# Moving one weight fetch, two pieces of product and some conversion steps in a fused attention and expert kernel

## The chip, the cores and the metric

The program runs on one core of a Trainium2 chip. The metric is device time in microseconds. The kernel before took a median of 728.87 us in three runs (727.69 to 729.34). Five engines work side by side, each through its own list of instructions in order: TensorE (PE, with its weight loads PEld), VectorE (DVE), ScalarE (ACT), GpSimd (POOL) and SyncE (SP), which here only issues DMAs. An instruction waits until the semaphores that it names have been reached, and everything behind it on its engine waits with it.

## The reference

Three stages, each fed by the one before. q, k and v have 2 batches of 8 heads, 768 rows and 64 columns; the gated layer has 512 inputs and 1536 hidden columns; there are 8 experts of 512 x 1024.

```python
# 1: attention; a row sees the rows of its own hash bucket
q_bits = (einsum('bhsd,dk->bhsk', q, proj) > 0); k_bits likewise
scores = where(q_bucket == k_bucket, q @ k.T / sqrt(D), -1e9)
attn = softmax(scores);  x = (attn @ v), heads side by side: 1536 x 512
# 2: gated layer
x = (x @ w_a) * (x @ w_b) @ w_out
# 3: each row goes to the one expert with the highest routing logit
out[mask] = gate_w[mask, None] * (relu(x[mask] @ w1[e]) @ w2[e])
```

## The kernel before

**Attention** runs in 48 units (NU = 48): 16 heads, three units each, a unit being two strips of 128 rows against all 768 columns. In the loop over u (`for u in range(NU + 2)`), unit u has its row maxima (L213, VectorE), exponentials (L219, ScalarE), normalisation (L231, GpSimd) and, two passes later, its 32x32 turn (L238, VectorE). TensorE makes the scores of the next unit (L205, L208) and then one of: half of a head's product with v (`pv`, L250, 48 matmuls that the trace shows as 96 records), the turning or signing of the next pair's q and k, or filler. The scores use two PSUM buffers (tag s), so those of the next strip wait for the exponential of the one before. Units 42 to 47 are the last pair of heads, 14 and 15.

**Filler** is the gated layer's first chunk. A piece is `gated_products(...)` for one half of the inner dimension, six matmuls of 128x384 (L536); two pieces make one product, whose result is read by L545 (ScalarE) or by L549, L550 and L551 (VectorE, ScalarE, GpSimd). `fill` tells in which pass how many pieces run. In passes 40, 43 and 46 they use PSUM banks of pv, later ones a buffer of the scores (then the output is named part). Until pass NU + 1 the reading steps are held back to the next pass's hook 2, behind its turn.

**Weights** of that chunk arrive as 64-bit numbers and are converted by `split64`: a fetch on SP (L431) and seven steps. With `scratch`, as here, these are rest (L436, VectorE), top (L439, VectorE), low (L445, ScalarE), add (L450, GpSimd), size (L455, ScalarE), guard (L461, VectorE) and parts (L466 on ScalarE, L467 on GpSimd). `outs` are the two halves of w_out. Both go through the tile late, which lies in the single buffer of raw, where the last pair's q and k had been loaded; the second half's fetch waits until the first half is converted. `plan` holds each fetch, `places` the passes of the seven steps.

The place within a pass is set by the hooks: in `hook(u, at)`, at 3 and 2 stand before and after the turn, 0 behind TensorE's work of the pass, 1 behind the fetch of v (`load_v`, four DMAs, L94), 4 at the end. Behind the loop the code goes on with hooks of passes NU + 2 to NU + 4, between which stand the two halves of head 15's product.

**Afterwards** the gated layer's products run chunk by chunk (ab, L536; yp, L568), the router is woven in, and the experts follow (hp, hr and op). SP fetches the next weights (raw) as buffers come free; the first of these, w_a, stands right behind late in its list. yp is the first product that reads the converted w_out.

The order of all instructions is that of the Python code: what a hook calls is put into each engine's list at that point.

Of the kernel before, what the change touches and what calls it, by code (L numbers as in the profile page):

```python
# [1030 lines left out]
def tile_kernel(ctx, tc, q, k, v, proj, w_a, w_b, w_out, emb, tau, w1, w2, out, dbg=None):  # L1031
    K = Kernel(tc, q, k, v, proj, w_a, w_b, w_out, emb, tau, w1, w2, out)
# [4 lines left out]
    with tc.manual_schedule():  # L1037
        const = ctx.enter_context(tc.tile_pool(name="const", bufs=1, side="left"))
        X = Experts(K, const)
# [12 lines left out]
        NU = B * H * (S // 256)  # L1052
        with tc.tile_pool(name="conv", bufs=1, side="left") as X.conv, \
                tc.tile_pool(name="att", bufs=2, side="right") as sb, \
                tc.tile_pool(name="ps_s", bufs=2, space=PSUM) as ps_s, \
                tc.tile_pool(name="ps_pv", bufs=1, space=PSUM) as ps_pv:

            def spare():
                return X.mid.tile([128, 4 * 384], F32R, tag="g", name="spare")

            def late():
                return sb.tile([128, 2 * S], F32, tag="raw", name="late", bufs=1)

            jobs = [X.load_first(w, f, spare) for f in range(2) for w in range(2)]
            outs = [X.load_first(2, f, late) for f in range(2)]


            plan = {(-1, 0): [jobs[0][0], jobs[1][0]], (36, 1): [outs[0][0]], (45, 1): [outs[1][0]]}
            places = (
                (3, 4, 5, 6, 6, 7, 9), (8, 8, 9, 10, 12, 13, 15), (16, 17, 18, 21, 21, 22, 27), (20, 23, 24, 28, 30, 31, 33),  # L1070
                (38, 38, 39, 40, 41, 41, 45), (NU, NU, NU, NU + 1, NU + 1, NU + 1, NU + 2),
            )
            for (_, steps), us in zip(jobs + outs, places):
                for m, u in enumerate(us):
                    plan.setdefault((u, 3 if m in (3, 4, 6) else 4), []).append(steps[m])
            plan[13, 0], plan[16, 0] = [jobs[2][0]], [jobs[3][0]]
            first = [(t, f, w, h) for t in range(2) for f in range(2) for w in range(2) for h in range(2)]


            fill = {40: 2, 43: 2, 46: 2, NU: 2, NU + 2: 2, NU + 3: 2, NU + 4: 4}  # L1080

            held = []

            def hook(u, at):
                if at == 2:
                    while held:
                        held.pop(0)()
                for job in plan.pop((u, at), []):
                    job()
                if at == 0:  # L1090
                    for n in range(fill.get(u, 0)):
                        t, f, w, half = first.pop(0)
                        if half == 0:
                            X.part = K.banks[(2, 0)[n // 2]] if u < NU else K.bank()
                        X.gated_products(0, t, f, w, half, X.part, held if u < NU + 2 else None)

            K.attention(X.xh, X.xl, (sb, ps_s, ps_pv), hook)
            assert not plan and not first
        pctx = ExitStack()
# [188 lines left out]
```

## Time and profile before

| | |
|---|---|
| median of three runs | 728.87 us (727.69 to 729.34) |
| profiled execution | 727.76 us |
| its span, first to last instruction | 726.0 us |
| PE busy | 697.9 us, 96% |
| PEld busy | 586.9 us, 81% |
| DVE busy | 459.0 us, 63% |
| POOL busy | 415.5 us, 57% |
| ACT busy | 354.1 us, 49% |
| mean share of DMA time of the bulk queue q1 | 37.5% |

The span lies 1.8 us under the execution's time. Times in the rows are from the span's start. Busy shares are means over stages that differ: up to some 232 us the attention runs, with filler, and behind it the gated layer and the experts. "Idle before" in a row is the time in which that engine did nothing before that instruction, and the name behind the arrow is what the profile takes to have ended the wait, which is inferred; "issue" means that it found nothing waited for.

### The profile page before, as it was taken

What the parts mean: (1) busy time and instruction counts of PE and PEld (TensorE: products, weight loads), DVE (VectorE), ACT (ScalarE), POOL (GpSimd) and SP (SyncE); (2) the same over time, 40 slices, a digit from 0 to 9 for tenths busy, and PEclk for the clock granted to TensorE, in tenths of its full rate; (3) what the DMA queues carried; (4) which work ended last, traced back from release to release, by engine and by line L of the source; (5) the groups of instructions that cost most, each with busy time, mean ns of one, the idle gap of its engine ahead of it and who ended that gap; (6) DMA issues with size and microseconds to landing.
All of it is one profiled execution on the core that took longest, in us unless ns stands there. A gap on an engine that the chain in (4) does not pass through costs nothing.

```text
span 726.0 us, 16193 instructions
## 1 busy us (share of the span) xinstructions
PE 697.9 (96%) x6793; PEld 586.9 (81%) x6793; DVE 459.0 (63%) x669; ACT 354.1 (49%) x658; POOL 415.5 (57%) x343
## 2 busy tenths in 40 slices
PE   7799999997989999999999999999999999999996
PEld 5455656564768989999999999998889899889995
DVE  3999999997984535646545556434744855555650
ACT  3778888886753342222121212143446556556551
POOL 0668778875773563745646626545424766656651
PEclk9999999999999999999999999999999999999999
DMA  6948744633341230311111301443332866577510
GB/s 143 220 111 177 162 119 117 164 84 98 71 133 60 72 105 5 113 59 58 59 60 59 112 4 59 157 162 116 113 134 79 290 215 219 196 240 241 202 54 23
DMA packets 68603, 88.29 MB, mean 122 GB/s; under 512 B 28963, under 2 KB 41123, under 8 KB 68528
## 3 DMA queue, kind: packets, MB, share of 16 engines
q1 hardware_dynamic: 63888, 78.71, 37.5%
q0 software_dynamic: 2560, 7.34, 2.7%
q10 hardware_dynamic: 2080, 1.18, 0.5%
q8 instruction: 54, 0.88, 0.5%
q14 instruction: 21, 0.17, 0.1%
HBM read 75.52 MB, written 7.34 MB: 114 GB/s over the span
## 4 chain that ended last, share of the span: by engine, by line
PE 77%; DVE 10%; ACT 5%; issue 3%; DMA 3%; POOL 1%; SPq 1%; POOLq 0%; DVEq 0%
PE ab L536 24%; PE yp L568 13%; PE op L912 11%; PE hp L862 10%; PE pv L250 6%; PE st L205 4%; DVE nm L213 4%; DVE et L238 3%; ACT e L219 3%; PE part L536 2%; PE hr L880 2%; PE xgt L839 1%; PE pv L536 1%; PE st L208 1%; DMA raw<-in_k_dram 1%
## 5 line engine op out<-in xcount | busy, mean ns | idle before, releaser
L536 PE MATMUL ab<-xh,w 128*128 128x384 f32 x704 | 185.7, 338 | 0.0
L536 PEld LDWEIGHTS ab<-xh,w 128*128 128x128 f32 x704 | 127.7, 188 | 2.1 <-issue 1.2
L231 POOL TENSOR_SCALAR e<-e,s,mc 128x768 f32<-128x768 f32 x96 | 93.8, 988 | 46.3 <-ACT e L219 38.2
L536 PE MATMUL ab<-xl,w 128*128 128x384 f32 x352 | 118.3, 336 | 0.0
L551 POOL TENSOR_TENSOR g<-a,g 128x384 fp32r<-128x384 f32 x48 | 56.4, 1176 | 107.2 <-ACT g L550 107.2
L818 POOL TENSOR_TENSOR w<-raw,w 128x1024 fp32r<-128x1024 f32 x36 | 88.0, 2447 | 39.2 <-ACT w L817 37.7
L568 PE MATMUL yp<-w,g 128*128 128x512 f32 x432 | 103.3, 391 | 1.0 <-DVE a L549 0.7
L219 ACT ACTIVATE e<-st,nm 128x768 f32<-128x768 f32 x96 | 85.8, 898 | 36.4 <-DVE r L223 25.7
L213 DVE TENSOR_REDUCE nm<-st 128x1 f32<-128x768 f32 x96 | 89.5, 937 | 11.2 <-PE st L208 10.8
L568 PEld LDWEIGHTS yp<-w,g 128*128 128x128 f32 x432 | 80.3, 188 | 16.6 <-DVE a L549 1.0
L205 PE MATMUL st<-ks,qs 64*128 64x384 f32 x192 | 83.7, 516 | 9.4 <-ACT e L219 9.1
L205 PE MATMUL st<-k,q 64*128 64x384 f32 x192 | 84.2, 519 | 4.6 <-ACT e L219 4.5
L238 DVE STREAM_TRANSPOSE et<-e 128x1536 f32<-128x1536 f32 x48 | 84.9, 1768 | 0.0
L912 PE MATMUL op<-w,hth 128*128 128x512 f32 x256 | 80.7, 397 | 0.0
L862 PE MATMUL hp<-xgh,w 128*128 128x256 f32 x448 | 80.7, 281 | 0.0
L250 PEld LDWEIGHTS pv<-et,vr 32*64 32x64 f32 x3072 | 60.7, 132 | 20.5 <-issue 11.1
L550 ACT CAST g<-a 128x384 fp32r<-128x384 f32 x48 | 24.7, 515 | 107.8 <-DVE a L549 107.8
L250 PE MATMUL pv<-et,vr 32*64 32x192 f32 x3072 | 72.7, 329 | 4.3 <-issue 2.3
L818 DVE TENSOR_TENSOR w<-raw,w 128x1024 fp32r<-128x1024 f32 x28 | 64.9, 2319 | 14.6 <-ACT w L817 14.3
L862 PEld LDWEIGHTS hp<-xgh,w 128*128 128x128 f32 x448 | 69.2, 188 | 0.3
L545 ACT COPY a<-ab 128x384 f32<-128x384 f32 x44 | 20.9, 476 | 95.6 <-PE ab L536 94.4
L536 PEld LDWEIGHTS ab<-xl,w 128*128 128x128 f32 x352 | 66.2, 188 | 0.8
(201 smaller groups left out, 1232.2 us busy)
## 6 DMA issues: line engine op xcount, KB each, us to landing
raw<-in_moe_w_dram SPq DMA_DIRECT2D x32, 1024.0 KB, 5.2
vr<-in_v_dram SPq DMA_DIRECT2D x64, 192.0 KB, 3.8
raw<-in_moe_w_a_dram SPq DMA_DIRECT2D x5, 1024.0 KB, 5.3
raw<-in_moe_w_b_dram SPq DMA_DIRECT2D x5, 1024.0 KB, 5.1
raw<-in_moe_w_out_dram SPq DMA_DIRECT2D x5, 1024.0 KB, 5.0
raw<-in_k_dram SPq DMA_DIRECT2D x16, 192.0 KB, 4.8
qs<-q SPq DMA_DIRECT2D x16, 192.0 KB, 3.7
raw<-in_q_dram SPq DMA_DIRECT2D x14, 192.0 KB, 4.1
```

The source lines that it names most:

```text
L205: nc.tensor.matmul(st[:, n, :H2], q[d, ql], k[d], start=True, stop=False, tile_position=(64 * n, 0))
L213: nc.vector.tensor_reduce(NM[u][:, t:t + 1], ST[u, t][:, :, :H2], axis=AX.XY, op=ALU.max, negate=True)
L219: nc.scalar.activation(halves(E[u][:, t]), ST.pop((u, t))[:, :, :H2], AF.Exp, bias=NM[u][:, t:t + 1], accum_out=SU[u][:, t:t + 1])
L231: nc.gpsimd.tensor_scalar(E[u][:, t], E[u][:, t], r[:, t:t + 1], c[:, t:t + 1], ALU.mult, ALU.add)
L238: nc.vector.transpose(ET[h][:, :, 2 * g:2 * g + 2].rearrange("p b c s -> p c b s"), E.pop(u).rearrange("p c (b s) -> p c b s", s=32),)
L250: nc.tensor.matmul(pvb[a // 2][m:m + 64, a % 2, :NC * 32], v[d], et[d, n].rearrange("p c s -> p (c s)"), start=(n < 2), stop=(n >= NB32 - ...
L536: nc.tensor.matmul(p[:, :384], w[:, k, fs], x[:, k, cols], start=(k == 0 and n == 0), stop=(k == self.KD - 1 and n == 2),)
L551: nc.gpsimd.tensor_tensor(gl[:, f], a, f32(gh[:, f]), ALU.subtract)
L568: nc.tensor.matmul(p, g[:, f, rows], w[:, f], start=(n == 0), stop=(n == 5))
L818: eng.tensor_tensor(l, raw, f32(h), ALU.subtract)
L862: nc.tensor.matmul(p[:, :256], w[:, k, fs], x[:, k], start=(n == 0), stop=(n == 3 * self.KD - 1))
L912: nc.tensor.matmul(p, h[:, 2 * n + f, rows], w[:, f], start=(n == 0 and f == 0 and m == 0), stop=(n == 3 and f == 1 and m == 2),)
```

## The change

In `tile_kernel`, five entries of tables change. The fetch of the first half of w_out goes from pass 36 to pass 35, and its first step, rest, from pass 38 to 37. The second half's steps top, low, add, size, guard and parts go one pass later each, its step rest and its fetch stay. Of the filler, the two pieces of pass NU + 2 go to pass 47, with a buffer of the scores as output; the pieces are taken in the same order as before, so pass 47 now runs those that pass 48 had, and pass 48 those that pass 50 had.

```diff
-            plan = {(-1, 0): [jobs[0][0], jobs[1][0]], (36, 1): [outs[0][0]], (45, 1): [outs[1][0]]}
+            plan = {(-1, 0): [jobs[0][0], jobs[1][0]], (35, 1): [outs[0][0]], (45, 1): [outs[1][0]]}
...
-                (38, 38, 39, 40, 41, 41, 45), (NU, NU, NU, NU + 1, NU + 1, NU + 1, NU + 2),
+                (37, 38, 39, 40, 41, 41, 45), (NU, NU + 1, NU + 1, NU + 2, NU + 2, NU + 2, NU + 3),
...
-            fill = {40: 2, 43: 2, 46: 2, NU: 2, NU + 2: 2, NU + 3: 2, NU + 4: 4}
+            fill = {40: 2, 43: 2, 46: 2, 47: 2, NU: 2, NU + 3: 2, NU + 4: 4}
...
-                            X.part = K.banks[(2, 0)[n // 2]] if u < NU else K.bank()
+                            X.part = K.banks[(2, 0)[n // 2]] if u < NU - 1 else K.bank()
```

On SP, at the last pair's swapped copies (ks, qs) and the fetch of head 12's v (vr), the lists differ so:

```order
 L106 DMA ks<-k 64x384 x2
 L104 DMA qs<-q 64x768 x2
+L431 DMA late<-in_moe_w_out_dram 128x1024
 L94 DMA vr<-in_v_dram 32x4x384 x4
-L431 DMA late<-in_moe_w_out_dram 128x1024
 L175 DMA qg<-qf 64x384 x2
 L94 DMA vr<-in_v_dram 32x4x384 x12
```

The fetch of late went from behind the four vr to ahead of them.

On VectorE, from the turn (L238) of unit 35 over pass 38 to the first row maximum of unit 39, before the change:

```order
L238 STREAM_TRANSPOSE et<-e 128x2x24x32
L213 TENSOR_REDUCE nm<-st 128x1
L223 RECIPROCAL r<-su 128x2
L213 TENSOR_REDUCE nm<-st 128x1
L229 SCALAR_TENSOR_TENSOR s_2744<-nm,r 128x2
L238 STREAM_TRANSPOSE et<-e 128x2x24x32
L436 TENSOR_SCALAR late<-late 128x512
L439 SCALAR_TENSOR_TENSOR late<-late 128x512
L213 TENSOR_REDUCE nm<-st 128x1
```

The same place after it:

```order
L238 STREAM_TRANSPOSE et<-e 128x2x24x32
L436 TENSOR_SCALAR late<-late 128x512
L213 TENSOR_REDUCE nm<-st 128x1
L223 RECIPROCAL r<-su 128x2
L213 TENSOR_REDUCE nm<-st 128x1
L229 SCALAR_TENSOR_TENSOR s_2745<-nm,r 128x2
L238 STREAM_TRANSPOSE et<-e 128x2x24x32
L439 SCALAR_TENSOR_TENSOR late<-late 128x512
L213 TENSOR_REDUCE nm<-st 128x1
```

L436, which reads what was fetched, went from behind the turn of unit 36 to behind that of unit 35; L439 stayed.

On TensorE, from head 14's products (L250) to the first filler matmul behind head 15's first half, the order's difference is (a filler product is 12 matmuls in nine such rows, part is its PSUM tile; the rows of filler in the middle are as they were):

```order
-L250 MATMUL pv<-et,vr 64x192 x96
+L250 MATMUL pv<-et,vr 64x192 x48
 L536 MATMUL part<-xh_98,w 128x384
 L536 MATMUL part<-xl_100,w 128x384
...
-L536 MATMUL part<-xh_98,w 128x384 x2
+L536 MATMUL part<-xh_98,w 128x384
+L250 MATMUL pv<-et,vr 64x192 x48
+L536 MATMUL part<-xh_98,w 128x384
```

Of the 24 filler matmuls that stood behind both halves of head 14, 12 now stand between the halves.

## Rows read from the trace of the kernel before

**Rows 1.** The page: engine, busy us (share) xinstructions; then one group of L250.

```profile
PE 697.9 (96%) x6793; PEld 586.9 (81%) x6793; DVE 459.0 (63%) x669; ACT 354.1 (49%) x658; POOL 415.5 (57%) x343
...
L250 PE MATMUL pv<-et,vr 32*64 32x192 f32 x3072 | 72.7, 329 | 4.3 <-issue 2.3
```

**Rows 2.** Stretches: from:to, length, busy us of each engine, PEclk, DMA share, GB/s.

```profile
170.00:174.00 4.00, 0.48 (x4) 0.35 (x6) 3.61 (x7) 1.52 (x3) 0.43 (x1) 1.00 0.01 1
174.00:180.00 6.00, 6.00 (x114) 3.50 (x112) 4.68 (x6) 3.52 (x9) 4.33 (x6) 0.72 0.01 3
212.00:214.50 2.50, 0.40 (x18) 0.38 (x20) 2.47 (x3) 0.00 (x0) 1.82 (x2) 1.00 0.09 31
214.50:219.50 5.00, 5.00 (x32) 4.72 (x20) 1.52 (x3) 2.77 (x6) 0.34 (x1) 0.66 0.01 3
232.50:726.00 493.50, 486.63 (x2867) 447.41 (x2867) 261.61 (x384) 186.63 (x314) 260.91 (x148) 1.00 0.36 118
```

**Rows 3.** Timeline of VectorE: start us, us, instruction, idle before and its releaser.

```profile
140.59 0.94 DVE L213 TENSOR_REDUCE nm<-st 128x1 f32<-128x768 f32 x1
...
151.77 0.96 DVE L213 TENSOR_REDUCE nm<-st 128x1 f32<-128x768 f32 x1 [0.31 <-PE st L208]
...
161.28 1.77 DVE L238 STREAM_TRANSPOSE et<-e 128x1536 f32<-128x1536 f32 x1
163.36 0.96 DVE L213 TENSOR_REDUCE nm<-st 128x1 f32<-128x768 f32 x1 [0.31 <-PE st L208]
...
170.36 0.43 DVE L436 TENSOR_SCALAR late<-late 128x512 int32<-128x512 int32 x1 [3.35 <-DMA qg<-qf]
...
180.28 0.96 DVE L213 TENSOR_REDUCE nm<-st 128x1 f32<-128x768 f32 x1 [1.38 <-PE st L208]
```

**Rows 4.** Timeline of SP's DMA issues: start us, us, DMA.

```profile
156.63 1.19 SPq L104 DMA_DIRECT2D qs<-q  x2
162.42 1.74 SPq L94 DMA_DIRECT2D vr<-in_v_dram  x4
164.20 0.43 SPq L431 DMA_DIRECT2D late<-in_moe_w_out_dram  x1
...
205.69 0.39 SPq L431 DMA_DIRECT2D raw<-in_moe_w_a_dram  x1
```

**Rows 5.** DMA from issue to landing: of qs, 157 to 160 us; of late.

```profile
qs<-q SPq DMA_DIRECT2D x2, 192.0 KB, 2.9
...
DMA to landing us min/median/max: 5.7/5.7/5.7
```

**Rows 6.** Chain of waits, 207 to 226 us: start us, us, what.

```profile
207.96 3.80 PE pv L250 x168
211.77 2.33 issue
214.10 0.87 PE pv L250 x20
214.96 5.94 PE part L536 x24
...
223.04 2.28 PE part L536 x12
```

**Rows 7.** DMA queues, 211 to 212 us: packets, MB, share of 16 engines.

```profile
q1 hardware_dynamic: 187, 0.37, 95.4%
q8 instruction: 1, 0.02, 6.1%
```

**Rows 8.** Instructions on tile late: duration ns min/median/max, first and last start us.

```profile
L436 DVE TENSOR_SCALAR late<-late x2: 427/748/1069, 170.4 to 211.0; 128x512 int32<-128x512 int32 x2
L439 DVE SCALAR_TENSOR_TENSOR late<-late x2: 694/1026/1357, 170.8 to 212.1; 128x512 int32<-128x512 int32 x2
```

**Rows 9.** Timelines of ScalarE and VectorE behind head 14's product.

```profile
215.01 0.48 ACT L270 COPY xp<-pv 64x384 f32<-64x384 f32 x1 [3.33 <-PE pv L250]
...
218.60 0.56 DVE L549 TENSOR_TENSOR a<-part,a 128x384 f32<-128x384 f32 x1 [3.48 <-PE part L536]
```

## The prediction

> **What bounds the kernel now.** I read the page's first section, then the table of stretches, then each engine's timeline around the two places that the diff touches, and the chain of waits last. TensorE is busy for 697.9 of 726.0 us [rows 1], and after 232.5 us for 486.63 of 493.5 us, at full clock [rows 2]. So what the attention stage saves is kept only if the later work shifts as a block; it can, since its first engine steps stand behind the attention's last ones, and TensorE is the engine that they feed. The attention stage has two holes in TensorE. In 170 to 174 us it is busy for 0.48 us, and in 212 to 214.5 us for 0.40 us; behind each hole comes a stretch at a granted clock of 0.72 and 0.66, between the two levels 1.2 and 2.4 GHz, so part of it ran at the low one [rows 2].
>
> The first hole comes from VectorE. Behind the turn of unit 36 (L238) it stands idle for 3.35 us and then runs L436 on tile late [rows 3]. The releaser in that row is qg, but L436 reads late: its fetch was issued at 164.20 us, behind the four vr fetches that SP could start only at 162.42 us [rows 4], and the late fetch whose landing is recorded took 5.7 us [rows 5]; 164.20 + 5.7 = 169.9, just ahead of 170.36. The next row maximum (unit 39) stands behind L436 and L439, so scores, exponentials and TensorE stop. Price: the first row maxima of units 32 and 35 start at 140.59 and 151.77 us, 11.18 us for three units; those of units 38 and 41 at 163.36 and 180.28 us, 16.92 us [rows 3]. The hole, its low clock and the two inserted steps cost 5.74 us.
>
> The second hole lies inside the products L250 of head 14: 168 of them, 2.33 us in which the row names nothing that was waited for ("issue"), then 20 more [rows 6]. In 211 to 212 us the bulk queue fills the 16 engines to 95.4% and one block of 16 KB passes on the instruction queue [rows 7]: the 1 MB of raw was issued at 205.69 us, next on SP behind the second late [rows 4]. I read the hole as TensorE waiting for its own code behind this traffic; over the whole program L250 has 2.3 us of such idle time, so this is the only one [rows 1]. It costs 2.33 us; the slow clock behind it makes 24 first-product matmuls take 5.94 us where 12 take 2.28, so 5.94 - 2 x 2.28 = 1.38 us, and 20 L250 take 0.87 instead of 20 x 3.80/168 = 0.45, so 0.42 us [rows 6]. Together 4.13 us.
>
> **The change part by part.** *Fetch a unit sooner.* In SP's order late now stands ahead of the four vr and right behind the two qs, which SP has issued by 156.63 + 1.19 = 157.8 us [rows 4]. vr loses nothing: it cannot start before 162.42. The landing is bounded by the rows of qs (2.9 us, 192 KB) and late (5.7 us, behind vr) [rows 5]: 160.7 to 163.5 us. L436 moved with it, to behind the turn of unit 35, which ends at 161.28 + 1.77 = 163.05 us [rows 3]. So its wait is 0 to 0.5 us; I take 0, since in the new place no vr is ahead of it.
>
> *L436 and L439 stay on VectorE*, now in two units. They cost 0.43 to 1.07 and 0.69 to 1.36 us [rows 8], the upper ones beside a busy GpSimd, less the 0.31 us that VectorE was idle at 163.36 us [rows 3]: 0.8 to 2.1 us. GpSimd is at work in both new places, and the unit's other engines have some slack, so I take 1.3. First term: 5.74 - 1.3 = 4.4 us, from 5.74 - 2.1 - 0.5 = 3.1 to 5.74 - 0.8 = 4.9.
>
> *Two pieces brought between the halves.* Twelve matmuls of 128x384 move from behind the second half of head 14's products to between its halves. The work is the same (five groups of 12 and four halves before yp, then as now), so all of the gain is the hole. TensorE ran the 168 L250 from 207.96 us; the first half has 92 of them left, to 207.96 + 92 x 0.0226 = 210.04 us. The pieces add 2.28, to 212.32. The code that was missing came at 214.10 us. If TensorE meets the same instruction count, it does so 12 matmuls earlier in the products: 160 instead of 172 of 192, that is 64 x 0.0226 = 1.45 us into the second half, at 213.77. The hole shrinks to 0.33 us, and with so short an idle I expect no low clock. Second term: 4.13 - 0.33 = 3.8 us. It can't be over 4.13; below, the fetch may be asked for later and land up to 1.2 us later, half of the room that the pieces fill: 2.6.
>
> What could be late next there: (a) The first half of head 15 needs the turn of unit 47. VectorE now runs L549 (0.56 [rows 9]) on the moved pieces, L436 (up to 1.07) and the turn (1.77 [rows 3]): 212.4 + 0.56 + 1.07 + 1.77 = 215.8 us. (b) It needs ScalarE's four copies L270 of head 14 (0.48 each [rows 9]): 214.82 + 1.95 = 216.8 us. TensorE gets to it at 214.10 + 32 x 0.0226 + 2.28 = 217.1 us with the next pieces. Both are covered, (b) by 0.3 us only. If (b) came later, TensorE would wait as long as it does.
>
> *Conversion steps of the second half* (L439, L445, L450, L455, L461) go a unit later. They and the two that make w from them work on 128x512 elements each; at L439's upper duration five of them in a row are 5 x 1.36 = 6.8 us [rows 8], and from the copies' end at 216.8 they would be done by 223.6. yp, which needs them, starts behind 217.1 + 2 x 2.17 + 3 x 2.28 = 228.3 us at the earliest. So I cost them at nothing; 4.7 us hide them, and what is over would delay yp. L439 now stands behind the turn of unit 47, which spares (a) its 0.69 to 1.36 us.
>
> *outs of the first half*: its L436 is the only step of it that moves.
>
> **Rule and row.** The row shows 2.33 us of TensorE idle with nothing waited for, and a code block passing amid a full bulk queue [rows 6, 7]. The Trainium skill, "Runtime: NRT & Kernel Launch", Instruction fetch mechanics, says that instructions come in 16 KiB blocks through a queue of the sequencer's own, and that crossing a block is mostly hidden. The trace agrees with the size (0.02 MB); with "mostly hidden" it would disagree if my reading holds. By that rule the hole is something else, which the pieces need not shrink; that is the first rival below.
>
> **Sum.** 4.4 + 3.8 = 8.2 us, and the later stage shifts whole. The profiled execution took 727.76 us, span 726.0, so it would take 719.6. It is 1.1 us below the median 728.87; against the median the forecast is 728.87 - 8.2 = 720.7 us. The forecast's own range: terms 3.1 to 4.9 and 2.6 to 4.13, so 5.7 to 9.0 us, 719.8 to 723.2; down to 718.7 if the profile's 1.1 us belong to the kernel.
>
> **Rivals.**
> Hole stays: if the 2.33 us and the slow clock come wherever TensorE runs a stretch of L250 there, only the first term is left: 728.87 - 4.4 = 724.5. For it: the row names no releaser. Against: it is the only one in 3072 products [rows 1], exactly when the bulk queue is full.
> Wait moves along: L436 stands a unit earlier as well; if late lands at 167 us, VectorE waits as long as before and only the second term is left: 728.87 - 3.8 = 725.1. For it: the load is 512 KB behind two qs. Against: [rows 5] bound the landing by 163.5.
> Change does nothing that shows: both of these, 728.9.
> Slower: code starves TensorE oftener. late now travels beside qs, right ahead of vr, and the 1 MB raw still follows the second late, with 12 more matmuls between TensorE and its next block. [rows 7] show what bulk on all engines can do to one block. Each hole costs 4.1 us as above. With the first two gone and three new ones the time is 728.87 - 8.2 + 3 x 4.1 = 733.0; from two on the change is no gain. Against: sixteen heads' vr were fetched, and L250 shows a single hole [rows 1].
>
> **How the numbers follow.** Forecast 0.66, hole stays 0.14, wait moves 0.08, nothing 0.07, slower 0.05. The first three are faster by over 0.2% (1.5 us, about what a measurement of this kernel can tell): 0.88; within it 0.07; slower 0.05. The range 718.7 to 725.2 takes in the first three.
>
> **What would show it.** After: L436 of the first half with under 0.6 us of idle before it, and the row maxima of units 38 and 41 some 12.5 us apart; granted clock 1.00 where it was 0.72. At the end: 12 first-product matmuls between two groups of 96 L250, and an "issue" of under 0.5 us in the second; yp starting some 8 us earlier than 232.5; about 493.5 us from there to the end. I am wrong if an idle of over 2 us stands in L250 again, if L436 waits over 2 us, or if the stage behind yp is over 1 us longer.

## The result, and the profile after

The changed kernel takes a median of 718.09 us in six runs (717.45 to 721.46); the kernel before, in six runs that include the three shown above, 727.97 us (724.78 to 729.34). The ratio is 0.988, with a 95% interval of 0.9849 to 0.9911: faster by some 9 us, where 8.2 us and a time of 720.7 us were forecast. The median lies 0.6 us below the forecast's range (718.7 to 725.2), which was worked out from the first three runs' 728.87 us; the ratio on that median gives 720.1 us, and the gain stands at the upper end of the 5.7 to 9.0 us forecast. The profiled execution took 717.86 us, its span is 716.1 us, 9.9 us under that of before.

The page after, engine by engine and the group L250, answers to [rows 1]:

```profile
PE 693.9 (97%) x6793; PEld 584.1 (82%) x6793; DVE 461.4 (64%) x669; ACT 353.8 (49%) x658; POOL 414.8 (58%) x343
...
L250 PE MATMUL pv<-et,vr 32*64 32x192 f32 x3072 | 71.7, 326 | 2.0 <-ACT q L128 1.9
```

L250 no longer has the 2.3 us of "issue". Stretches after (columns as in [rows 2]), around the two places and from yp's start on:

```profile
160.00:180.00 20.00, 19.35 (x376) 12.13 (x361) 19.79 (x29) 17.05 (x36) 15.40 (x20) 1.00 0.42 106
200.00:223.50 23.50, 22.74 (x456) 19.67 (x456) 13.68 (x21) 10.91 (x23) 13.07 (x14) 1.00 0.43 130
223.50:716.00 492.50, 486.06 (x2867) 447.51 (x2867) 264.58 (x384) 186.54 (x314) 260.38 (x148) 1.00 0.36 119
```

TensorE works for 19.35 of 20 us and 22.74 of 23.5 us, at full clock, where it had the two holes and a granted clock of 0.72 and 0.66. Behind yp's start it does the same 486 us of work. VectorE's timeline, to be held against [rows 3]:

```profile
151.44 0.96 DVE L213 TENSOR_REDUCE nm<-st 128x1 f32<-128x768 f32 x1 [0.31 <-PE st L208]
...
160.94 1.77 DVE L238 STREAM_TRANSPOSE et<-e 128x1536 f32<-128x1536 f32 x1
162.74 0.71 DVE L436 TENSOR_SCALAR late<-late 128x512 int32<-128x512 int32 x1
163.37 0.94 DVE L213 TENSOR_REDUCE nm<-st 128x1 f32<-128x768 f32 x1
...
166.92 1.06 DVE L439 SCALAR_TENSOR_TENSOR late<-late 128x512 int32<-128x512 int32 x1
...
175.13 0.96 DVE L213 TENSOR_REDUCE nm<-st 128x1 f32<-128x768 f32 x1
```

The rows at 163.37 and 175.13 us are the first maxima of units 38 and 41: 11.76 us apart, where it was 16.92. L436 has no idle time before it. SP's issues after, which answer to [rows 4]:

```profile
156.31 1.19 SPq L104 DMA_DIRECT2D qs<-q  x2
157.60 0.54 SPq L431 DMA_DIRECT2D late<-in_moe_w_out_dram  x1
162.08 1.74 SPq L94 DMA_DIRECT2D vr<-in_v_dram  x4
...
200.54 0.39 SPq L431 DMA_DIRECT2D raw<-in_moe_w_a_dram  x1
```

The view of the tile does not tell when this fetch landed after the change. It does so for the same fetch in the kernel after with a store (one of the experiments below), where it was issued at 157.34 us (KB, then us from issue to landing):

```profile
late<-in_moe_w_out_dram SPq DMA_DIRECT2D x1, 512.0 KB, 5.0
```

By that, late landed at about 157.60 + 5.0 = 162.6 us; in the trace of after itself the semaphore of this fetch was last raised at 162.56 us. That lies inside the 160.7 to 163.5 us forecast, but only 0.15 us ahead of the end of unit 35's turn at 160.94 + 1.77 = 162.71 us, behind which L436 starts. The chain of waits at the end of the attention, for [rows 6]:

```profile
202.81 2.20 PE pv L250 x92
205.01 2.28 PE part L536 x12
207.29 2.34 PE pv L250 x96
209.63 2.28 PE part L536 x12
211.91 2.13 PE pv L250 x96
...
218.47 4.38 PE part L536 x24
...
223.56 4.38 PE yp L568 x18
```

Twelve matmuls of filler stand between head 14's two halves, no "issue" is left, and 24 of filler take 4.38 instead of 5.94 us. The second half takes 2.34 us where the next takes 2.13: that is what is left of the hole. The code block still passes amid a full bulk queue; the DMA queues from 206 to 207 us, as in [rows 7]:

```profile
q1 hardware_dynamic: 191, 0.38, 97.5%
q8 instruction: 1, 0.02, 6.5%
```

**Where the 9.9 us came from.** I cut both traces at the first row maximum of units 35, 38, 41 and 47 and at yp's first matmul; the last three columns are from the experiments below. All in us:

| stretch | before | after | fetch and rest | pieces | steps |
|---|---|---|---|---|---|
| start to unit 35 | 151.77 | 151.44 | 151.02 | 151.22 | 152.00 |
| units 35 to 38 | 11.59 | 11.94 | 11.94 | 11.59 | 11.59 |
| units 38 to 41 | 16.92 | 11.76 | 11.76 | 18.10 | 16.41 |
| units 41 to 47 | 24.05 | 24.04 | 24.02 | 24.02 | 24.02 |
| unit 47 to yp | 28.22 | 24.38 | 27.96 | 24.90 | 26.40 |
| yp to the end | 493.43 | 492.51 | 492.41 | 492.64 | 492.24 |

The first hole gave 16.92 - 11.76 - 0.35 = 4.81 us, the second 28.22 - 24.38 = 3.84. Both are figures of one pair of executions: other traces that keep the first hole (pieces, steps and, below, the store in the kernel before) took 18.10, 16.41 and 17.36 us for units 38 to 41, by which it is worth 4.3 to 6.0 us. The other 1.25 us stand in the first and the last stretch. The start varies by 1 us between these traces without a change that reaches it, and the end is as short with the steps alone, which win nothing that can be measured; so I don't count them to the change.

### The profile page after: what moved, and what is told of

Same layout as the page of the kernel before. It is cut to its first block, busy times and chain, and to the rows that moved or that the text cites. A ratio compares the mean times of both kernels' runs of the same rounds, so it can differ in the third digit from the quotient of the medians.

```text
span 716.1 us, 16191 instructions
## 1 busy us (share of the span) xinstructions
PE 693.9 (97%) x6793; PEld 584.1 (82%) x6793; DVE 461.4 (64%) x669; ACT 353.8 (49%) x658; POOL 414.8 (58%) x343
## 4 chain that ended last, share of the span: by engine, by line
PE 78%; DVE 11%; ACT 4%; issue 3%; DMA 3%; SPq 0%; POOL 0%; POOLq 0%; DVEq 0%
PE ab L536 25%; PE yp L568 14%; PE op L912 11%; PE hp L862 10%; PE pv L250 5%; DVE nm L213 5%; PE st L205 4%; DVE et L238 4%; ACT e L219 2%; PE hr L880 2%; PE part L536 2%; PE xgt L839 1%; PE pv L536 1%; PE st L208 1%; DMA raw<-in_k_dram 1%
## 5 line engine op out<-in xcount | busy, mean ns | idle before, releaser
L551 POOL TENSOR_TENSOR g<-a,g 128x384 fp32r<-128x384 f32 x48 | 51.4, 1070 | 102.5 <-ACT g L550 102.3
L238 DVE STREAM_TRANSPOSE et<-e 128x1536 f32<-128x1536 f32 x48 | 84.9, 1768 | 0.0
L250 PEld LDWEIGHTS pv<-et,vr 32*64 32x64 f32 x3072 | 59.7, 130 | 17.6 <-issue 8.2
L250 PE MATMUL pv<-et,vr 32*64 32x192 f32 x3072 | 71.7, 326 | 2.0 <-ACT q L128 1.9
```

The lines of the kernel that those rows point to most:

```text
L238: nc.vector.transpose(ET[h][:, :, 2 * g:2 * g + 2].rearrange("p b c s -> p c b s"), E.pop(u).rearrange("p c (b s) -> p c b s", s=32),)
L250: nc.tensor.matmul(pvb[a // 2][m:m + 64, a % 2, :NC * 32], v[d], et[d, n].rearrange("p c s -> p (c s)"), start=(n < 2), stop=(n >= NB32 - ...
L551: nc.gpsimd.tensor_tensor(gl[:, f], a, f32(gh[:, f]), ALU.subtract)
```

## The experiments

My theory: there are two holes apart from each other, the first of VectorE waiting for late, the second of TensorE waiting for its own code behind bulk traffic; the fetch heals the one, the pieces heal the other. The rivals: qg, which the profile names, held VectorE; moving the steps did it; the second hole belongs to that run of products, whatever the traffic.

The diffs show parts of the changed lines.

**Fetch and rest alone.**

```diff
-(36, 1): [outs[0][0]]
+(35, 1): [outs[0][0]]
-(38, 38, 39, 40, 41, 41, 45)
+(37, 38, 39, 40, 41, 41, 45)
```

> Only the first half's fetch (pass 36 to 35) and its step rest (38 to 37). Theory (two separate holes, each part of the change removes one): the first hole goes, 4.8 us of the trace's 9.9 us; ratio about 0.9935; the issue hole inside L250 of head 14 stays at 1.5 to 2.5 us, yp starts 4.5 to 5.5 us earlier than 232.5. Rival (the two holes are one story, the late start of attention's end makes the second): the second hole shrinks too, and the gain is 7 us or more.

720.96 us against 726.8 (the median of before in this and the next three experiments), ratio 0.9914 [0.9899, 0.9930]. Units 35 to 41 go as after, to 0.01 us. The gain is above what I expected: 0.9935 lies outside the interval, and yp started at 226.69 us, 5.85 us sooner; beyond the first hole the trace is shorter in the start, behind unit 47 and behind yp (table), where the edit moves nothing. The second hole comes earlier by the time saved, and stays whole; its chain of waits:

```profile
202.38 3.80 PE pv L250 x168
206.18 2.08 issue
208.26 0.87 PE pv L250 x20
209.12 5.93 PE part L536 x24
```

So the holes are independent.

**Pieces alone.**

```diff
-fill = {40: 2, 43: 2, 46: 2, NU: 2, NU + 2: 2, NU + 3: 2, NU + 4: 4}
+fill = {40: 2, 43: 2, 46: 2, 47: 2, NU: 2, NU + 3: 2, NU + 4: 4}
-X.part = K.banks[(2, 0)[n // 2]] if u < NU else K.bank()
+X.part = K.banks[(2, 0)[n // 2]] if u < NU - 1 else K.bank()
```

> Only the two pieces, brought between the halves of head 14's product. Theory: the first hole stays as before (L436 idle 3 to 3.5 us before it), the second shrinks to under 0.5 us; 3.4 to 3.9 us less, ratio about 0.995. VectorE now has L549, L436 and L439 ahead of the turn of unit 47, which may cost up to 0.5 us of it. Rival (the hole comes wherever TensorE runs L250 there): an issue of about 2.3 us stands in L250 again, ratio 1.000.

722.84 us, 0.9940 [0.9925, 0.9955]. The first hole stays (18.10 us from unit 38 to 41), the second shrinks to 0.47 us in the chain:

```profile
210.76 2.28 PE part L536 x12
213.04 1.49 PE pv L250 x64
214.52 0.47 issue
214.99 0.91 PE pv L250 x32
215.90 2.28 PE part L536 x12
```

The hole now comes after 64 products of the second half, the place where 0.33 us of idle were worked out. Before the break TensorE ran 92 + 12 + 64 = 168 matmuls, and in [rows 6] 168 as well: the break goes by the count of instructions, so the 12 of filler bring it 12 products earlier. Counted from the program's start, the break stands before the same matmul, the 3655th recorded, in before and in every experiment that has it in L250. The queue of the blocks carries 54 of them in each trace, one for some 252 of TensorE's 2 x 6793 matmuls and weight loads [rows 1]: that it is TensorE's own code is read from these counts.

**Conversion steps alone.**

```diff
-(NU, NU, NU, NU + 1, NU + 1, NU + 1, NU + 2),
+(NU, NU + 1, NU + 1, NU + 2, NU + 2, NU + 2, NU + 3),
```

> Only the second half's conversion steps a pass later. Theory: hidden, ratio 0.999 to 1.001, both holes as before. Rival (they are what lets the turn of unit 47 and so head 15 come earlier): 1 us or more less on their own.

725.54 us, 0.9989 [0.9975, 1.0003]: no difference that can be told. Both holes stand. In its chain, though, the filler behind the second one is quick:

```profile
211.47 2.08 issue
213.55 0.87 PE pv L250 x20
214.42 4.36 PE part L536 x24
```

```profile
213.50:219.00 5.50, 5.45 (x60) 4.90 (x68) 2.02 (x3) 3.47 (x8) 1.01 (x1) 1.00 0.01 3
```

The second fence is the stretch behind that hole: its granted clock is 1.00. So a hole of this length is followed by a low clock in some executions and not in others; with the low clock the same 24 matmuls took 5.94 us, 1.58 more. What decides it stays open. And the 20 products took 0.87 us at full clock too, so that this part of the price isn't the clock's.

**Rest alone**, the rival that qg was the releaser: L436 a pass sooner with the fetch where it was.

```diff
-(38, 38, 39, 40, 41, 41, 45)
+(37, 38, 39, 40, 41, 41, 45)
```

> Only the step rest a pass sooner, with its fetch left behind the four vr. Theory (VectorE's order with the landing of late is the first hole): L436 now waits in pass 37 until about 170 us, for some 6.5 to 7 us, ahead of the row maximum of unit 38; 2 to 4 us slower, ratio 1.003 to 1.006. Rival (what ended the wait was qg's landing, as the row named it): L436 now stands ahead of the qg fetch in the program, so the wait goes and 4 us are gained.

730.62 us, 1.0041 [1.0027, 1.0056]: slower. VectorE's timeline, and late's fetch, which was issued at 163.68 us (us to landing last):

```profile
170.72 0.43 DVE L436 TENSOR_SCALAR late<-late 128x512 int32<-128x512 int32 x1 [8.19 <-DMA late<-in_moe_w_out_dram]
...
late<-in_moe_w_out_dram SPq DMA_DIRECT2D x1, 512.0 KB, 6.8
```

L436 starts at 170.72 us, as in [rows 3], though it stands a unit sooner in the list: the landing of late, at 163.68 + 6.8 = 170.5 us, sets it, not qg. The idle time grew to 8.19 us, more than the 6.5 to 7 expected.

**Fetch alone**, with rest where it was.

```diff
-(36, 1): [outs[0][0]]
+(35, 1): [outs[0][0]]
```

> Only the first half's fetch a pass sooner, its step rest left in pass 38. Theory (the landing was all that the first hole waited for): as with rest moved too, within 0.6 us of it: ratio 0.990 to 0.994, L436 without idle before it, second hole as before. Rival (moving L436 a pass ahead was needed): half of the gain or less.

723.41 us against 726.71 (the median of before here and in the rest), 0.9958 [0.9943, 0.9972]. VectorE no longer waits for late, but does both steps in one unit:

```profile
166.93 0.82 DVE L436 TENSOR_SCALAR late<-late 128x512 int32<-128x512 int32 x1
167.79 1.37 DVE L439 SCALAR_TENSOR_TENSOR late<-late 128x512 int32<-128x512 int32 x1
169.08 0.94 DVE L213 TENSOR_REDUCE nm<-st 128x1 f32<-128x768 f32 x1
```

TensorE's timeline shows what that costs: 1.21 us of idle before the next scores, where after has 0.38.

```profile
171.16 0.59 PE L205 MATMUL st<-ks,qs 64*128 64x384 f32 x1 [1.21 <-ACT e L219]
```

From unit 38 to 41 it takes 12.94 us, with rest moved as well 11.76, less 0.35 in the three units before: 0.83 us by the traces. The second hole stayed, at 2.30 us. My expectation of within 0.6 us of fetch and rest together missed: the move of rest spreads the two steps over two units. The rival's "half of the gain or less" isn't met by the medians either: 3.30 us against 5.84. The medians and the spans (721.6 and 719.1) differ by 2.5 us, though; the other 1.7 stand in the start (151.78 against 151.02), unit 47 to yp (28.16 against 27.96) and behind yp (493.10 against 492.41), where the edit moves nothing. Their cause stays open.

**Less traffic at the block, in the kernel before.** SP first stores 64 x 4 values of what ScalarE copies from head 14's product, which it has to wait for, so that the 1 MB of raw is issued after the hole's place, at 215.71 us. The tile mark, in the chip's DRAM, is new too.

```diff
+                if u == NU + 1: nc.sync.dma_start(out=self.mark, in_=XP[len(pairs) - 1][0][0:64, 0:4])
```

> The kernel before, with SP held in front of the 1 MB raw by a 1 KB store of what ScalarE copies from head 14's product (about 215 us). The order on the other engines is that of before. Theory (the second hole is TensorE waiting for its code behind the bulk of late and raw): the code block passes by 210.5 instead of 211.8 us, the hole in L250 shrinks from 2.1 to 2.3 us to 0 to 0.9 us; the first hole stays; 1.5 to 3.5 us less, ratio 0.995 to 0.998. Rival (a stretch of 192 products makes the hole by itself): a hole of 2 us or more, ratio 1.000.

723.59 us, 0.9952 [0.9939, 0.9966]. TensorE's instructions and their order are those of before; the chain of waits:

```profile
208.70 3.80 PE pv L250 x168
212.51 0.25 issue
212.75 0.87 PE pv L250 x20
213.62 4.36 PE part L536 x24
```

The DMA queues, 210 to 211 us, in which the block passes:

```profile
q1 hardware_dynamic: 38, 0.09, 24.0%
q8 instruction: 1, 0.02, 6.9%
```

The same break after the same 168 products lasts 0.25 us instead of 2.33 [rows 6], with the bulk queue at 24.0 instead of 95.4% [rows 7]. The block began to pass at 210.41 us, 1.71 us behind the products' start at 208.70; in the kernel before at 211.78, 3.82 us behind 207.96. It came 2.11 us sooner, and the hole shrank by 2.08. This settles the second hole: it is code that comes late behind bulk. Of the rival, that the products make the hole by themselves, 0.25 us are left.

Why it stands just here can be estimated, though no run varies it alone. At some 252 instructions, a block holds some 126 matmuls with their weight loads. The products run through those in 126 x 0.0226 = 2.8 us, hardly more than the 2.34 us that passed here from the block's start (210.41) to TensorE's going on (212.75); filler, at 2.28 us for 12, would need some 24 us [rows 6]. So the 192 products in a row leave next to no room for a late block, and 12 matmuls of filler between the halves leave 2.28 us more.

**The same store in the kernel after.**

```diff
+                if u == NU + 1: nc.sync.dma_start(out=self.mark, in_=XP[len(pairs) - 1][0][0:64, 0:4])
```

> The changed kernel with the same hold of SP. Theory: the pieces already cover the code block, at most 0.2 us of a hole is left to win; within 0.5 us of the changed kernel, ratio to before 0.985 to 0.990. Rival (the bulk still slows TensorE or the other engines there): another 1 us or more is won.

718.56 us, 0.9890 [0.9874, 0.9906], as after. raw went out at 211.30 us, 10.8 us later, and a small hole came with it to a later place, inside the filler:

```profile
217.99 1.42 PE part L536 x7
219.41 0.60 issue
220.01 3.14 PE part L536 x17
```

The block that holds this place passed from 217.74 us on, and TensorE went on 2.27 us after that. The break lies 255 matmuls, two blocks, behind the former one; raw passed just ahead of it, on a bulk queue that filled 73.2% of the engines from 214 to 217.5 us.

**More traffic at a block, in the kernel after**: 1.57 MB of unused weights are fetched behind vr in pass 36.

```diff
+plan[36, 1] = [lambda: nc.sync.dma_start(out=spare().bitcast(I32), in_=w_a.bitcast(I32)[:128, :1536])] * 2
```

> The changed kernel with two useless fetches of 0.79 MB each into the idle filler buffers, issued behind head 12's vr in pass 36. Theory (bulk ahead of a code block starves TensorE): the block that the changed kernel fetched at 166.4 us comes at 168.5 to 171 us, and a hole with no named releaser, 0.5 to 3 us, appears in TensorE in 168 to 175 us, where there was none; 0.5 to 4 us slower than the changed kernel. Rival (code blocks pass by the bulk): no such hole, the same time as the changed kernel within 0.5 us.

717.80 us, 0.9876 [0.9861, 0.9892]: as after, and the hole that I expected did not come. The trace shows why: the block of that place passed from 168.09 us on, 1.65 us later than in after (166.44), but TensorE has no idle time there but one of 0.38 us behind ScalarE's exponentials, which after has too: it still had code when the block was in. By the count of instructions, an estimate, some 180 were left when this block began to pass, where at the hole of before one was left. (At the old place of the second hole this trace has 0.21 us of "issue".) Bulk traffic delays a block (here the bulk queue filled 98.0% of the engines from 166.4 to 168 us); whether that makes a hole depends on how much code TensorE has left.

No version came out ahead of the changed kernel: the last two are equal to it within their intervals.

## Why the prediction was right, step by step

- **The first hole**: right in its cause and place (fetch and rest alone; rest alone as the counter-test). The term was 4.4 us, measured 4.81, and 4.3 to 6.0 against the other traces with the hole. The inserted steps were put at 1.3 us beyond an 11.18 us pace of three units, 12.5 in all; units 38 to 41 took 11.76, and units 35 to 38 0.35 more. What is too small is the value of moving rest: I counted both steps as if they cost the same wherever they stand, while apart they cost 0.83 us less than together.
- **The landing** of late at 160.7 to 163.5 us: 162.56, and no wait. But it is covered by 0.15 us only; a landing late in the forecast's own span would have cost up to 0.8 us, so that the wait was 0 is in part luck. The rival "wait moves along" is out for this kernel; rest alone shows what it would have looked like, and that it would have been dearer than I wrote: slower than before, not only the term lost.
- **The second hole**: 3.8 us forecast, 3.84 measured. That the break goes by the count of instructions holds (pieces alone: after 64 products, 0.47 us against the 0.33 worked out). In the kernel after, no idle was left, only 0.21 us in 96 products. Of its parts the 0.42 us of slow products are not the clock's, as the steps alone show, and the 1.38 us of slow filler come only in some executions. The rival "hole stays" is out by pieces alone and by the store in the kernel before.
- **Covers**: the first half of head 15 began at 211.91 us. (a) The turn of unit 47 ended at 208.20 + 1.77 = 209.97 us, 1.94 us ahead (1.3 by the forecast's sums). (b) ScalarE's last copy L270 of head 14 ended at 211.19 + 0.48 = 211.67: covered by 0.24 us, 0.3 forecast. It was thin, and it held. The rows:

```profile
208.20 1.77 DVE L238 STREAM_TRANSPOSE et<-e 128x1536 f32<-128x1536 f32 x1
...
211.19 0.48 ACT L270 COPY co<-pv 64x384 f32<-64x384 f32 x1
```

- **Conversion steps** at nothing: right (0.9989, with 1 inside the interval).
- **yp and behind**: it started 8.98 us earlier (some 8 forecast), of which 0.33 are the start's. The stage behind it took 492.51 us (about 493.5 forecast).
- **The rival "slower"**: the block still passes at 97.5% of bulk, yet no third hole came. Its point of decision was misjudged: not the traffic alone, but the code that TensorE has left.
- **The rule** of the Trainium skill, "Runtime: NRT & Kernel Launch", Instruction fetch mechanics, that crossing a block is mostly hidden: the trace of before disagrees at this one place (2.33 us) and agrees at the other blocks of TensorE's L250, where there is no such idle time [rows 1].

The two parts alone gained 5.84 and 3.96 us, 9.8 together; the changed kernel 9.9 in its own runs, and with the store or the extra fetch 8.2 and 8.9 (against 726.71): within the intervals, the parts add up.

## What to carry to other kernels

An idle time for which the profile names no releaser can be the engine's own code, late behind bulk DMA: look at which queue passes an instruction block there, and either keep bulk out of those microseconds or put other work, of longer instructions, before the break. A named releaser is a guess where an instruction waits for several things or waits in turn: look up what the instruction reads, and when that was issued and landed. When a stalled load is brought forward, see whether its consumers can be placed apart too (0.83 us here); the consumer brought forward alone cost 3.8 us.

## What the runs showed of the hardware that was not expected

- TensorE goes on only 2.26 to 2.51 us after its block began to pass, in all nine traces that have such a hole (before: 211.78 to 214.10 us; with the store in the kernel after: 217.74 to 220.01). That was the same beside 95.4% of bulk [rows 7] and 9.1% (217 to 219 us of the latter trace). What the traffic moves is when the block begins to pass.
- The granted clock behind a hole of 2.1 to 2.3 us fell in some traces (0.66 in [rows 2]) and stayed at 1.00 in another (the steps alone). From unit 47 to yp such a hole cost 28.22 - 24.38 = 3.84 us with the low clock and 26.40 - 24.38 = 2.02 without.
- 1.57 MB of bulk ahead of a block cost nothing that can be measured (717.80 us) where TensorE still had code left.
